# First expert group's rows transposed inside the last two attention chunks, with their buffers placed over the finished k, v and q buffers

## The chip, the cores and the metric

The kernel runs on one core of one Trainium2 chip. The core has five engines: TensorE (PE in the profile), VectorE (DVE), ScalarE (ACT), GpSimd (POOL) and SyncE (SP), and 16 DMA engines that move data. The metric is the device time of one execution in microseconds, lower being better. Time before: a median of 1042.11 us over 3 runs, from 1041.54 to 1044.14.

## What is computed

Two parts, the second on the output of the first. The attention has 8 batches, 8 heads, 576 positions of 64 values; keys and values are averaged over 8 positions first:

```python
k_p = k.reshape(B, H, Sp, pool, D).mean(axis=3)      # pool = 8, Sp = 72
v_p = v.reshape(B, H, Sp, pool, D).mean(axis=3)
scores = scale * np.matmul(q, k_p.transpose(0, 1, 3, 2))
attn = softmax(scores)
x = np.matmul(attn, v_p)                             # laid out as 4608 rows of 512
```

The mixture of experts takes these 4608 rows. A noisy gate picks the best two of 8 experts for each row, and each expert is a network of two layers, 512 to 1024 to 512:

```python
noisy = x @ w_gate + log1p(exp(x @ w_noise)) * noise
top2, top2_w = best two of noisy, softmax over the two
out[row] = sum over its two experts e of  top2_w * (relu(x[row] @ w1[e]) @ w2[e])
```

## The kernel before

**Attention.** A loop runs over 36 chunks of 128 rows: 4 pairs of batches (`pr` 0 to 3), 9 chunks each (`ci`). Chunks belong to units; a unit is two chunks (`jj` 0 and 1) or one. For a chunk `et` (lines 372 to 388) transposes the exponentials on PE (L385, four into a PSUM tile of tag `one`, two into the end of the chunk's accumulator `a`) and copies them on ACT to SBUF (`eT`, L387, with a raised priority); `av` (lines 390 to 428) multiplies with the values (12 matmuls, L399), divides on DVE (`rd` L405 and L406, `xr` L410, `lg` L412) and writes the rows to DRAM (`x_dram`, L417 and L420). Scores of the next unit come from `qk` (L361, maximum L366, exponential L368), and the q rows of the unit after it from `qtr` (L335). The last two chunks, 34 and 35, are the two halves of the last unit; no unit follows, so there is only `et` and `av` in them.

**Routing.** After each 9 chunks `route` (from line 477) works out on DVE and ACT which experts the rows go to, beginning with a sum over the heads (L495), ranks them by matmuls (L568, L572), and queues 18 scatters on POOL (L597) that write row numbers and weights into lists in DRAM (`rec_dram`), one list for each expert. `load_recs` (L612 on) reads lists back (`raw`, L628): the first expert's tiles 0 to 3 after half of the pairs, its tiles 4 to 6 after the third pair, both on POOL's queue, and all the rest on SP's queue once the last pair's scatters have landed. From the last load POOL converts row numbers (`x` L670, `xf` L648), and 16 small matmuls spread them over partitions (`px` and `pw`, L642); they stand in PE's order behind the sixth of the eight blocks of the second group's first layer. Rows are fetched with indirect DMAs on POOL (`xg`, L689 for the first expert).

**Experts.** Each expert's list is worked off in three groups of up to 512 rows. `split` transposes the group's rows (for the first expert on PE, L905, 4 transposes for each of up to 4 tiles of 128 rows) and splits the values into a high part `xh` (ACT cast, first half of L916) and a low part `xl` (DVE subtraction, same line). `stage1` runs 8 blocks (f = 0 to 7) of 12 matmuls (L956) and evicts each with ACT (`hh`, L961) and DVE (`hl`, L962); a matmul reads the columns of all tiles of the group at once. For the first group and f = 0 the matmuls that read `xh` come first (8), then those that read `xl` (4). `stage2` is the second layer (L1060, L1031). Weights are loaded into three staging buffers (`wst`, L446) and split in the same way by `weights` (ACT L467, DVE L468), four steps for a weight tile; a staging buffer is loaded again when its two steps are done.

**The seam.** Two weight tiles of the first expert, `weights(0, 0)` and `weights(0, 1)`, are split during the last pair by the generator `early_w`: eight steps, six in chunks 30 to 32, and the last two behind the loop (`drain(early_w)`). Then the attention's pools close (`att` in SBUF, `ps2` in PSUM), the experts' pools open over the same addresses (`moe`, `mps`, each tile waiting only for the tiles it lies over), and `split(groups[0])` begins. In block f = 0 and after, `hook0` takes up the last pair's `route` and weight tiles 2 and 3. Behind the load of the last of these pieces, on SP's queue, stand 12 writes of zeros to `out` (L936, 768 KB each), and behind those three loads for the second expert's weights and then the late `raw` loads.

**Order.** A planner orders each engine's instructions: by priority, which is the order in which the code traces them, among those whose operands it takes as ready. `tc.issue_after(i)` holds instructions behind `i` on `i`'s engine. Each engine works its own list in order.

Of the kernel before, what the change touches and what calls it, by code (L numbers as in the profile page):

```python
# [20 lines left out]
def kernel(  # L21
# [91 lines left out]
    ctx2 = ExitStack()  # L113
    ap_ = ctx2.enter_context(tc.tile_pool(name="att", bufs=1))
    ps2 = ctx2.enter_context(tc.tile_pool(name="ps2", bufs=1, space=PSUM))
    ps2.tile([P, 512], F32, tag="s", name="s_first", bufs=2)

    ZW = 3
# [88 lines left out]

    def kvload(dst, src, b, nm, nb, np_, parts, acc):

        t = ap_.tile([P, nb, PD], F32, tag=nm, name=f"{nm}{b}", bufs=2)  # L210
        r = src[b].rearrange("h (g t) d -> (h g) (t d)", t=POOL)
        for n0, n1, r0, st in parts:
            def ld(o, w, eng, **kw):
                eng.dma_start(t[:np_, n0:n1, :w], bass.AP(
                    tensor=r.tensor, offset=r.offset + r0 * PD + o,
                    ap=[[PD, np_], [st * PD, n1 - n0], [1, w]]), **kw)
            if acc >> b & 1:
                ld(0, HD, nc.sync)
                accs.append(lambda ld=ld: ld(HD, HD, nc.gpsimd, accum_op=OP.add))
            else:  # L220
                ld(0, PD, nc.sync)
        dst[b] = t
# [25 lines left out]
               [(n, n + 2, VSR[n], VSR[n + 1] - VSR[n]) for n in range(0, NEB, 2)], DV)  # L248

    def load_q(b):  # L250
        t = ap_.tile([P, H, 4, D], F32, tag="q", name=f"q{b}", bufs=2)
        for h in range(0, H, H // (QS if b == 0 else 1)):
            hs = slice(h, h + H // (QS if b == 0 else 1))
            nc.sync.dma_start(t[:, hs].rearrange("p h j d -> p h (j d)"),
                              q[b, hs, :4 * P, :].rearrange("h (p j) d -> p h (j d)", j=4))
        QT[b] = t
        if b % 2 == 0:
            QR[b // 2] = ap_.tile([P, H, D], F32, tag="qr", name=f"qr{b}", bufs=2)
        nc.sync.dma_start(QR[b // 2][b % 2 * 64:b % 2 * 64 + 64],
                          q[b, :, 4 * P:, :].rearrange("h p d -> p h d"))  # L260

    KS, VS, QTT, EX, XR = {}, {}, {}, {}, {}

    def k_prep(b):
        ks = ap_.tile([P, NB, 2, D], F32, tag="ks", name=f"ks{b}")
        KS[b] = ks
        for n0, n1 in ((0, 2), (2, 4), (4, 5)) if b == 0 else ((0, NB),):
            yield from pooled(ks[:, n0:n1], KT[b], n0, n1, P)
# [102 lines left out]
    def et(u, jj):  # L371
        kind, pr, b, jp = u
        nm = f"{pr}_{b}_{jp}_{jj}"
        ex = EX[u][:, jj]
        eT = ap_.tile([P, NEB, P], F32, tag="eT", name=f"eT{nm}", bufs=2)

        a = ps2.tile([P, 2, 512], F32, tag="a", name=f"a{nm}", bufs=AB)
        for n0, n1 in EG:
            if n0:
                ep = a[:, :, 512 - P:]  # L380
            else:
                ep = ps2.tile([P, 512], F32, tag="one", name=f"ep{nm}_{n0}", bufs=2).rearrange(
                    "p (n t) -> p n t", t=P)
            for n in range(n0, n1):
                nc.tensor.transpose(ep[:BST, n - n0], ex[:, ES[n]:ES[n] + BST], ident)  # L385
            with tc.high_priority(offset=HP):
                lastt[0] = nc.scalar.copy(eT[:BST, n0:n1], ep[:BST, :n1 - n0])  # L387
        return eT, a
# [86 lines left out]
    def drain(g):  # L475
        for _ in g:
            pass
# [232 lines left out]
    def one(name):  # L710
        return ps2.tile([P, 512], F32, tag="one", name=name, bufs=2)

    units = []
    for pr in range(NP):
        units += [("D", pr, 2 * pr, 0), ("D", pr, 2 * pr, 1), ("R", pr, 2 * pr, 2),
# [106 lines left out]
    for i, (ui, u, jj) in enumerate(chunks):  # L822
# [5 lines left out]
        if single:  # L828
            order = OR
        else:  # L830
            order = OD[jj]
        eT = None
        def bgs():
            for f in bg.get(i, ()):
# [5 lines left out]
        for o in order + ("" if "b" in order else "b") + ("" if "x" in order else "x"):  # L840
            if o == "v" and i == 0:
                drain(pg[0])
            if o == "b":
                bgs()
            elif o == "x":
                adv()
            elif o == "e":
                eT, at = et(u, jj)
            elif o == "v":
                av(u, jj, ci, eT, at, lgs[pr])  # L850
                lx[i] = lastx[0].ins
            elif o in "012":
                if has:
                    qk(units[ui + 1], int(o))
            elif ui + 2 < NU:
                qtr(units[ui + 2], "qr".index(o))
# [13 lines left out]
            gens.append(route(pr, 0, 5, lgs[pr], one))  # L870
        if ci == NCH - 1 and pr < NP - 1:
            gens.append(route(pr, 5 if pr >= HS else 0, NCH, lgs[pr], one))
    advance(100, 100)
    with tc.issue_after(lastt[0].ins), tc.issue_after(lx[len(chunks) - 2]):
        drain(early_w)
    ctx2.close()


    mctx = ExitStack()
    mp = mctx.enter_context(tc.tile_pool(name="moe", bufs=1, reuse_waits="tile"))  # L880
    pools.append(mp)
    mps = mctx.enter_context(tc.tile_pool(name="mps", bufs=1, space=PSUM, reuse_waits="tile"))

    def w1s(e, hl, db, f):
# [3 lines left out]
        return W[e, 2 + f // 4][:, hl, (f % 4) * DM:(f % 4 + 1) * DM]  # L888

    PASSES = ((0, 0), (0, 1), (1, 0))  # L890
    XT = {}
    SP_ = [None]

    def split(grp):
        e, t0, nt = grp
        xh = mp.tile([P, NDB, 4 * P], F32R, tag="xh", name=f"xh{e}_{t0}")
        xl = mp.tile([P, NDB, 4 * P], F32R, tag="xl", name=f"xl{e}_{t0}")
        for t in range(nt):
            xg = XG.pop((e, t0 + t))
            if e == 0:  # L900
                xp = mps.tile([P, NDB, P], F32, tag="xp", name=f"xp{e}_{t0 + t}", bufs=2) if t0 + t not in (2, 3) else \
                    mps.tile([P, NDB, P], F32, tag="ph", name=f"xp{e}_{t0 + t}", bufs=3)
                xv = xg.rearrange("p (c b) -> p b c", b=NDB)
                for db in range(NDB):
                    nc.tensor.transpose(xp[:, db], xv[:, db], ident)  # L905
                nr = 2 if t0 + t == 9 else 4
                xT = xp.rearrange("p b (r j) -> p b r j", j=32)[:, :, :nr]
            else:
                nr = 2 if t0 + t == 9 else 4
                xt = mp.tile([P, 4, NDB, 32], F32, tag="xt", name=f"xt{e}_{t0 + t}", bufs=2)  # L910
                nc.vector.transpose(xt[:, :nr], xg[:, :nr * P].rearrange("p (r i b) -> p r b i", i=32, b=NDB))
                xT = xt.rearrange("p r b j -> p b r j")[:, :, :nr]
            cs = slice(t * P, t * P + nr * 32)
            xhv = xh[:, :, cs].rearrange("p b (r j) -> p b r j", j=32)
            xlv = xl[:, :, cs].rearrange("p b (r j) -> p b r j", j=32)
            SP_[0] = (nc.scalar.copy(xhv, xT), nc.vector.tensor_sub(xlv, xT, xhv.bitcast(F32)))  # L916
        XT[grp] = (xh, xl)

    HT = {}
    hli = {}  # L920
    evict = []
# [156 lines left out]
                except StopIteration:  # L1078
                    wgens.pop(0)

    with tc.high_priority(offset=LP):
        split(groups[0])
    s0 = SP_[0]
    fetch(groups[1])
    rt = route(NP - 1, 0, NCH, lgs[NP - 1], mone)

# [175 lines left out]
```

## Time and profile before

| What | Value |
|---|---|
| median of 3 runs | 1042.11 us (1041.54 to 1044.14) |
| profiled execution | 1041.25 us |
| its span, first to last instruction | 1039.1 us, so 2.15 us lie around it |
| mean granted TensorE clock | 0.992 |
| PE busy | 1015.6 us, 98% of the span |
| POOL, DVE, ACT busy | 632.6, 560.3 and 338.7 us |
| DMA moved | 140.63 MB, mean 135 GB/s |

A row of the timeline gives start and duration in us, engine, source line, operation, what is written from what, how many were merged, and in brackets the idle time of the engine before it with what ended it. A row of the table of stretches gives the stretch, each engine's busy time in it (with its number of instructions), the granted clock as a share of full speed, the mean busy share of the 16 DMA engines, and GB/s. SPq is SP's queue: there a duration is the time that issuing took, not the transfer.

### The profile page before, as it was taken

The page shows a single profiled execution, that of the slowest core. Times are in us where ns is not written, and L with a number is a line of the kernel's source. Part 1 is how long each engine was busy: PE and PEld are TensorE (multiplying, and loading weights), DVE is VectorE, ACT ScalarE, POOL GpSimd, SP SyncE. Part 2 cuts the span into 40 slices and gives each one's busy share as a digit, 9 for nine tenths or more (in the row PEclk, how much of TensorE's full clock was granted, in tenths as well). Part 3 has the DMA queues.
Part 4 walks back from the last instruction along what each step waited for, and adds up shares of the span by engine and source line. Part 5 has one row for each costly group of instructions (what it writes and reads, how often), then busy time and mean ns, then how long its engine had stood idle before and what let it go on. Part 6 is the DMA issues. An engine that isn't in the chain of part 4 may idle for free. (4 is left out here: it accounts for less than half of the span.)

```text
span 1039.1 us, 16032 instructions
## 1 busy us (share of the span) xinstructions
PE 1015.6 (98%) x5872; PEld 917.8 (88%) x5872; DVE 560.3 (54%) x1284; ACT 338.7 (33%) x857; POOL 632.6 (61%) x661
## 2 busy tenths in 40 slices
PE   6999999999999999999999999999999999999997
PEld 5898998788998998899889988998899889988995
DVE  6898987823464545454545464446444644554331
ACT  5787787412222232123212222222222222222110
POOL 4005476565677677677757775777577757773541
PEclk8999999998999999999999999999999999999999
DMA  9999936796234424442444243423442444232200
GB/s 299 312 329 276 257 82 174 264 213 174 81 92 134 134 65 119 123 141 70 117 130 132 67 123 112 139 72 117 121 124 84 114 122 121 79 93 84 69 19 32
DMA packets 76292, 140.63 MB, mean 135 GB/s; under 512 B 24501, under 2 KB 32778, under 8 KB 76212
## 3 DMA queue, kind: packets, MB, share of 16 engines
q1 hardware_dynamic: 47892, 76.82, 26.3%
q0 software_dynamic: 28320, 62.77, 20.0%
q8 instruction: 47, 0.77, 0.3%
q14 instruction: 33, 0.27, 0.1%
HBM read 102.27 MB, written 39.17 MB: 136 GB/s over the span
## 5 line engine op out<-in xcount | busy, mean ns | idle before, releaser
L956 PE MATMUL ph<-xh,w 128*128 128x384 f32 (+2 forms) x1536 | 405.6, 345 | 0.7 <-ACT xh L916 0.7
L697 POOL DMA_INDIRECT xg<-x_dram,x x266 | 259.3, 975 | 101.9 <-issue 68.9
L956 PEld LDWEIGHTS ph<-xh,w 128*128 128x128 f32 x1536 | 275.7, 188 | 21.2 <-ACT xh L916 0.9
L961 ACT ACTIVATE hh<-ph 128x512 fp32r<-128x512 f32 (+2 forms) x192 | 97.5, 509 | 564.4 <-PE ph L956 564.4
L1060 PE MATMUL py<-w,hh 128*128 128x512 f32 x896 | 276.6, 390 | 0.0
L956 PE MATMUL ph<-xl,w 128*128 128x320 f32 (+2 forms) x768 | 264.5, 345 | 0.0
L962 DVE SCALAR_TENSOR_TENSOR hl<-ph,hh 128x512 fp32r<-128x512 f32 (+2 forms) x192 | 111.0, 579 | 221.9 <-ACT hh L961 221.8
L1060 PEld LDWEIGHTS py<-w,hh 128*128 128x128 f32 x896 | 167.9, 188 | 34.5
L1060 PE MATMUL py<-w,hl 128*128 128x512 f32 x448 | 174.5, 389 | 0.0
L956 PEld LDWEIGHTS ph<-xl,w 128*128 128x128 f32 x768 | 144.7, 188 | 10.3
L998 DVE SCALAR_TENSOR_TENSOR pv<-py,raw,pv 128x128 f32<-128x128 f32 x196 | 54.9, 343 | 131.0 <-PE py L1060 130.4
L1031 PE MATMUL py<-hh,w 128*128 128x320 f32 x512 | 112.8, 309 | 0.0
L1045 POOL DMA_INDIRECT out_dram<-pv,o x80 | 84.6, 1058 | 36.0 <-issue 14.6
L1060 PEld LDWEIGHTS py<-w,hl 128*128 128x128 f32 x448 | 84.1, 188 | 17.4
L1019 POOL DMA_INDIRECT pv<-out_dram,o x70 | 72.4, 1034 | 35.6 <-issue 17.4
L597 POOL DMA_INDIRECT rec_dram<-rec,pos x72 | 74.6, 1036 | 29.5 <-issue 19.2
L1002 POOL DMA_INDIRECT out_dram<-pv,raw x56 | 58.9, 1052 | 53.5 <-DVE pv L998 33.3
L468 DVE TENSOR_TENSOR w<-wst,w 128x512 fp32r<-128x512 f32 x128 | 87.7, 688 | 4.5 <-ACT w L467 4.0
L1031 PEld LDWEIGHTS py<-hh,w 128*128 128x128 f32 x512 | 85.6, 188 | 0.0
L467 ACT CAST w<-wst 128x512 fp32r<-128x512 f32 x128 | 77.2, 615 | 6.4 <-DMA wst<-in_moe_w_dram 3.5
L1031 PE MATMUL py<-hl,w 128*128 128x320 f32 x256 | 79.1, 309 | 0.0
L980 POOL DMA_INDIRECT pv<-out_dram,raw x49 | 50.1, 1022 | 39.4 <-issue 39.4
(157 smaller groups left out, 1003.7 us busy)
## 6 DMA issues: line engine op xcount, KB each, us to landing
wst<-in_moe_w_dram SPq DMA_DIRECT2D x64, 512.0 KB, 3.9
v<-in_v_dram SPq DMA_DIRECT2D x24, 448.0 KB, 11.1
out_dram<-lg SPq DMA_DIRECT2D x12, 768.0 KB, 17.2
k<-in_k_dram SPq DMA_DIRECT2D x7, 1280.0 KB, 13.4
q<-in_q_dram SPq DMA_DIRECT2D x7, 1024.0 KB, 15.0
x_dram<-xr POOLq DMA_DIRECT2D x12, 512.0 KB
xg<-x_dram,x POOLq DMA_INDIRECT x276
x_dram<-xr SPq DMA_DIRECT2D x4, 512.0 KB, 7.0
```

The source lines that it names most:

```text
L467: nc.scalar.copy(hv, sv)
L468: nc.vector.tensor_sub(lv, sv, hv.bitcast(F32))
L597: s = nc.gpsimd.indirect_dma_start(out=rec_dram[:, :], out_offset=bass.IndirectOffsetOnAxis(ap=pos[:, i, c:c + 1], axis=0), in_=rec[:, c, ...
L697: nc.gpsimd.indirect_dma_start(out=xg[:, r * P:(r + 1) * P], out_offset=None, in_=x4, in_offset=bass.IndirectOffsetOnAxis(ap=xi[e, t][:, r ...
L956: nc.tensor.matmul(ph[:, :n], w1s(e, a, db, f), xs[b][:, db, :n], start=(i == 0), stop=(i == 3 * NDB - 1))
L961: ra = nc.scalar.activation(hh[:, :n], ph[:, :n], AF.Relu)
L962: rd = hli[grp, f] = nc.vector.scalar_tensor_tensor(hl[:, :n], ph[:, :n], 0.0, hh[:, :n].bitcast(F32), op0=OP.max, op1=OP.subtract)
L1002: s = nc.gpsimd.indirect_dma_start(out=out, out_offset=bass.IndirectOffsetOnAxis(ap=tokc[e, t][:np_], axis=0), in_=res[:np_], in_offset=No ...
L1019: g = nc.gpsimd.indirect_dma_start(out=pv4[:, i], out_offset=None, in_=out4, in_offset=bass.IndirectOffsetOnAxis(ap=oi4[e, t0 + i // 4][:, ...
L1031: nc.tensor.matmul(py[:, :n], w2s(e, b, f)[:, mb * P:(mb + 1) * P], hs[f][a][:, :n], start=(i == 0), stop=(i == 3 * NFB - 1))
L1045: s = nc.gpsimd.indirect_dma_start(out=out4, out_offset=bass.IndirectOffsetOnAxis(ap=oi4[e, t0 + i // 4][:, i % 4], axis=0), in_=r4[:, i], ...
L1060: lastm[0] = nc.tensor.matmul(py, hs[f][a][:, cs], w2s(e, b, f), start=(i == 0), stop=(i == 3 * NFB - 1))
```

## The change

The buffers for k, v, q and the pooled keys (`k`, `v`, `q`, `qr`, `ks`) move from the pool `att` into a pool of their own, `kvq`, opened after it. When chunk 34 begins, `kvq` closes, and a pool `xpose` opens at the other end of SBUF, for `xh` and `xl` alone. The first group's tile 0 is transposed and split in chunk 34 between `et` and `av`, its tiles 1 to 3 in chunk 35 at the same place; their PSUM tiles carry the attention's tags, `s` (tiles 0 and 1) and `one` (tiles 2 and 3), and no longer the experts'. The two remaining steps of `early_w` are parted: one as before, the other behind the split of tile 3 on ACT and DVE. `split` itself is cut into `xtiles` and `split_tile`, and the later groups use it as before. The diff, cut to its core:

```diff
+    ctx3 = ExitStack()
+    kp = ctx3.enter_context(tc.tile_pool(name="kvq", bufs=1))
...
-        t = ap_.tile([P, nb, PD], F32, tag=nm, name=f"{nm}{b}", bufs=2)
+        t = kp.tile([P, nb, PD], F32, tag=nm, name=f"{nm}{b}", bufs=2)
...
-        t = ap_.tile([P, H, 4, D], F32, tag="q", name=f"q{b}", bufs=2)
+        t = kp.tile([P, H, 4, D], F32, tag="q", name=f"q{b}", bufs=2)
...
-        ks = ap_.tile([P, NB, 2, D], F32, tag="ks", name=f"ks{b}")
+        ks = kp.tile([P, NB, 2, D], F32, tag="ks", name=f"ks{b}")
...
+    def xtiles(grp):
+        return [pools[-1].tile([P, NDB, 4 * P], F32R, tag=w, name=f"{w}{grp[0]}_{grp[1]}") for w in ("xh", "xl")]
+
+    def split_tile(grp, t, xs, xp=None):
+        e, t0, nt = grp
+        xh, xl = xs
+        xg = XG.pop((e, t0 + t))
+        nr = 2 if t0 + t == 9 else 4
+        if e == 0:
+            xv = xg.rearrange("p (c b) -> p b c", b=NDB)
+            for db in range(NDB):
+                nc.tensor.transpose(xp[:, db], xv[:, db], ident)
+            xT = xp.rearrange("p b (r j) -> p b r j", j=32)[:, :, :nr]
...
+        SP_[0] = (nc.scalar.copy(xhv, xT), nc.vector.tensor_sub(xlv, xT, xhv.bitcast(F32)))
...
+        if i == len(chunks) - 2:
+            ctx3.close()
+            pools.append(mctx.enter_context(tc.tile_pool(name="xpose", bufs=1, side="right", reuse_waits="tile")))
+            x0 = xtiles(groups[0])
...
                 eT, at = et(u, jj)
+                for t in {len(chunks) - 2: (0,), len(chunks) - 1: (1, 2, 3)}.get(i, ()):
+                    split_tile(groups[0], t, x0, ps2.tile([P, NDB, P], F32, tag="s" if t < 2 else "one",
+                                                          name=f"xp{t}", bufs=2))
...
+    XT[groups[0]] = x0
+    s0 = SP_[0]
     advance(100, 100)
     with tc.issue_after(lastt[0].ins), tc.issue_after(lx[len(chunks) - 2]):
+        next(early_w)
+    with tc.issue_after(s0[0].ins), tc.issue_after(s0[1].ins):
         drain(early_w)
     ctx2.close()
...
-    pools.append(mp)
+    pools.insert(0, mp)
...
-    with tc.high_priority(offset=LP):
-        split(groups[0])
-    s0 = SP_[0]
```

## Rows read from the trace of the kernel before

**Rows 1.** Timeline of PE, 172 to 200 us, columns as told above: the seam

```profile
175.77 1.78 PE L399 MATMUL a<-vbd,eT 112*128 112x162 f32 x12 [0.46 <-ACT eT L387]
...
178.23 1.78 PE L399 MATMUL a<-vbd,eT 112*128 112x162 f32 x12 [0.46 <-ACT eT L387]
179.84 2.11 PE L905 MATMUL xp<-ident,xg 128*128 128x128 f32 x16
182.65 2.11 PE L956 MATMUL ph<-xh,w 128*128 128x512 f32 x8 [0.70 <-ACT xh L916]
```

**Rows 2.** Timeline of ACT at the seam

```profile
177.80 0.37 ACT L387 COPY eT<-a 112x256 f32<-112x256 f32 x1 [1.38 <-PE a L385]
...
180.54 2.05 ACT L916 CAST xh<-xp 128x512 fp32r<-128x512 f32 x4 [1.33 <-PE xp L905]
```

**Rows 3.** Timeline of DVE at the seam

```profile
177.66 0.17 DVE L405 TENSOR_SCALAR rd<-a 128x8 f32<-128x8 f32 x1 [1.44 <-PE a L399]
...
178.90 1.28 DVE L468 TENSOR_TENSOR w<-wst,w 128x512 fp32r<-128x512 f32 x2
...
181.33 2.47 DVE L916 TENSOR_TENSOR xl<-xp,xh 128x512 fp32r<-128x512 f32 x4
183.72 2.12 DVE L495 TENSOR_REDUCE rt<-lg 128x144 f32<-128x1152 f32 x1
...
190.65 0.22 DVE L534 TENSOR_TENSOR rt<-rt,rt 128x72 f32<-128x72 f32 x1
```

**Rows 4.** Timeline of PE, 150 to 172.5 us: the last transposes of q

```profile
161.59 1.04 PE L335 MATMUL qp<-ident,q 128*128 128x128 f32 x8
```

**Rows 5.** Timeline of PE around 243 us

```profile
243.10 0.78 PE L642 MATMUL px<-xf,sel 128*128 128x80 f32 x3 [2.21 <-POOL xf L648]
```

**Rows 6.** Timeline of POOL, 186 to 275 us

```profile
191.75 0.59 POOL L628 DMA_DIRECT2D raw<-rec_dram  x1 [2.43 <-DMA rec_dram<-rec,pos]
197.33 0.69 POOL L667 TENSOR_SCALAR x<-raw 128x3 int32<-128x3 int32 x1 [4.99 <-DMA raw<-rec_dram]
...
202.29 1.01 POOL L597 DMA_INDIRECT rec_dram<-rec,pos  x1 [0.30 <-DVE cum L1164]
...
225.05 0.96 POOL L597 DMA_INDIRECT rec_dram<-rec,pos  x1 [0.91 <-DMA out_dram<-lg]
...
242.40 0.33 POOL L670 TENSOR_SCALAR x<-raw 128x3 int32<-128x3 int32 x1 [11.53 <-DMA raw<-rec_dram]
242.79 0.25 POOL L648 CAST xf<-raw 128x80 f32<-128x80 int32 x1
```

**Rows 7.** Timeline of SP's queue, 176 to 275 us (issues)

```profile
181.25 0.34 SPq L420 DMA_DIRECT2D x_dram<-xr  x1
190.76 0.37 SPq L446 DMA_DIRECT2D wst<-in_moe_w_dram  x1
191.18 21.91 SPq L936 DMA_DIRECT2D out_dram<-lg  x12
...
235.55 5.02 SPq L628 DMA_DIRECT2D raw<-rec_dram  x4
```

**Rows 8.** Table of stretches, columns as told above: DMA while zeros are written

```profile
193.00:202.00 9.00, 9.00 (x49) 7.30 (x48) 8.72 (x36) 3.87 (x8) 3.76 (x4) 1.00 1.01 379
...
210.00:226.00 16.00, 16.00 (x78) 13.47 (x77) 5.32 (x15) 1.66 (x3) 11.60 (x12) 1.00 1.08 202
```

**Rows 9.** Table of stretches: the clock behind 243 us

```profile
242.00:244.00 2.00, 0.90 (x5) 0.91 (x6) 0.65 (x2) 0.00 (x0) 1.37 (x4) 0.82 0.01 0
244.00:246.00 2.00, 2.00 (x11) 2.00 (x11) 0.55 (x1) 0.00 (x0) 1.45 (x2) 0.50 0.87 72
...
250.00:252.00 2.00, 2.00 (x12) 2.00 (x12) 0.56 (x1) 0.49 (x1) 1.70 (x2) 0.97 0.69 260
```

**Rows 10.** Table of stretches: PE from 243 us to its last matmul

```profile
243.00:1031.00 788.00, 787.90 (x4179) 712.56 (x4180) 374.63 (x749) 184.89 (x360) 524.62 (x522) 1.00 0.35 103
```

**Rows 11.** Timeline of POOL, 157 to 162 us: the first load of a list

```profile
160.37 0.24 POOL L667 TENSOR_SCALAR x<-raw 128x4 int32<-128x4 int32 x1 [0.92 <-DMA raw<-rec_dram]
```

More of the change, by code (lines that the diff above doesn't have):

```diff
@@ L257, in load_q @@
         if b % 2 == 0:
-            QR[b // 2] = ap_.tile([P, H, D], F32, tag="qr", name=f"qr{b}", bufs=2)
+            QR[b // 2] = kp.tile([P, H, D], F32, tag="qr", name=f"qr{b}", bufs=2)
         nc.sync.dma_start(QR[b // 2][b % 2 * 64:b % 2 * 64 + 64],
@@ L711, in one, with split @@
         return ps2.tile([P, 512], F32, tag="one", name=name, bufs=2)
+    mctx = ExitStack()
+    XT = {}
+    SP_ = [None]
+    def xtiles(grp):
[10 more added lines that the diff above has]
+            xT = xp.rearrange("p b (r j) -> p b r j", j=32)[:, :, :nr]
+        else:
+            xt = pools[0].tile([P, 4, NDB, 32], F32, tag="xt", name=f"xt{e}_{t0 + t}", bufs=2)
+            nc.vector.transpose(xt[:, :nr], xg[:, :nr * P].rearrange("p (r i b) -> p r b i", i=32, b=NDB))
+            xT = xt.rearrange("p r b j -> p b r j")[:, :, :nr]
+        cs = slice(t * P, t * P + nr * 32)
+        xhv = xh[:, :, cs].rearrange("p b (r j) -> p b r j", j=32)
+        xlv = xl[:, :, cs].rearrange("p b (r j) -> p b r j", j=32)
+        SP_[0] = (nc.scalar.copy(xhv, xT), nc.vector.tensor_sub(xlv, xT, xhv.bitcast(F32)))
+    def split(grp):
+        XT[grp] = xtiles(grp)
+        for t in range(grp[2]):
+            split_tile(grp, t, XT[grp],
+                       mps.tile([P, NDB, P], F32, tag="xp", name=f"xp{grp[1] + t}", bufs=2) if grp[0] == 0 else None)
     units = []
@@ L872 @@
             gens.append(route(pr, 5 if pr >= HS else 0, NCH, lgs[pr], one))
+    XT[groups[0]] = x0
+    s0 = SP_[0]
     advance(100, 100)
     with tc.issue_after(lastt[0].ins), tc.issue_after(lx[len(chunks) - 2]):
+        next(early_w)
+    with tc.issue_after(s0[0].ins), tc.issue_after(s0[1].ins):
         drain(early_w)
     ctx2.close()
-    mctx = ExitStack()
     mp = mctx.enter_context(tc.tile_pool(name="moe", bufs=1, reuse_waits="tile"))
-    pools.append(mp)
+    pools.insert(0, mp)
     mps = mctx.enter_context(tc.tile_pool(name="mps", bufs=1, space=PSUM, reuse_waits="tile"))
@@ L890 @@
     PASSES = ((0, 0), (0, 1), (1, 0))
[L891 to L917, printed above, removed]
     HT = {}
```

## Prediction

> **What bounds the kernel now.** The page gives PE 98% of the span, so I first ask where PE stands still, in its timeline. There are six idle stretches of over 0.25 us behind 150 us. Three lie at the seam between attention and experts: 0.46 us ahead of chunk 34's `av`, 0.46 ahead of chunk 35's, and 0.70 between the transposes of the first group and its first matmul [rows 1], together 1.62 us. Two more, under 0.5 us each, lie ahead of the seam and are not touched. The last is 2.21 us at 243.1, where the matmul that spreads the row numbers waits for POOL's `xf` [rows 5]. Behind that the table of stretches has PE busy for 787.90 of 788 us [rows 10], and the tail after PE's last matmul hangs on PE. So the end of the kernel is set by **when the matmul at 243.1 may start**. PE's work ahead of it is slack, 2.21 us of it.
>
> What releases that matmul is read backwards. `xf` (242.79) follows the last load of the lists, for which POOL waited 11.53 us [rows 6]. SP issued this load at 235.55, behind the 12 writes of zeros (191.18 to 213.1) [rows 7]. In that time the 16 DMA engines are full: mean busy share 1.01 and 1.08, with 379 GB/s until POOL's scatters begin and 202 GB/s beside them [rows 8]. The release is thus the end of a pile of transfers that starts with the zeros. The zeros follow a weight load (190.76) in SP's order, and that one follows the splitting of the staging buffer, which DVE ends at 190.65 [rows 3, 7].
>
> **The change part by part.** *Transposes on PE.* The 16 transposes take 2.11 us, 0.53 us a tile [rows 1]. They are as many as before. Tile 0 now stands ahead of chunk 34's `av`, and 0.53 us of work meets an idle 0.46 us there. Tiles 1 to 3 (1.58 us) stand ahead of chunk 35's `av`, in its idle 0.46 us. When `av` of chunk 35 is over, the first group's matmuls follow at once, if `xh` is there: chunk 35's `et` transposes ended at 178.23 - 0.46 = 177.77 and end 0.07 later now (0.53 - 0.46), tile 3 is transposed 1.58 us after that, at 179.42, and `av` needs 1.61 us (178.23 to 179.84) up to 181.03. ACT needs 0.51 us a tile [rows 2] and one weight half besides, and is done by 180.5. So the first matmul of the experts moves from 182.65 to 181.03, the whole 1.62 us. The other end: if the planner puts tile 3 behind `av`, the 0.70 stays and 0.92 is gained. I take 1.62, since the transposes come first in the code and need nothing that is late.
>
> *Waits that it adds.* A transposed tile needs its PSUM bank. Tiles 0 and 1 wait for exponentials, tiles 2 and 3 for the copies of `eT`; behind them in PE's order stands only `av`, which waits for the later copy (177.80) [rows 2] anyway. The new SBUF pool lies over k, v, q and `ks`; the last transposes of q ran at 161.59 [rows 4], 12 us earlier, so this costs nothing. The expert buffers slide down by the size of that pool, and weight tile 3 of the first expert lies now over `eT` and `xr`, whose last write to DRAM is issued at 181.25 [rows 7]; `hook0` fills that tile from block f = 2 on, over 8 us later, so I put it at nothing.
>
> *DVE and the start of the zeros.* DVE has no idle time from 177.66 to the routing's first sum at 183.72: two chunks' divisions, two weight halves (1.28 us), four subtractions (2.47 us, 0.62 each) [rows 3]. That work stays. Only tile 0's subtraction can slip into the 1.44 us that were idle ahead of 177.66, so the routing starts 0.62 us earlier; if the second weight half (0.64) falls behind the sum, 1.26. DVE stays busy up to 190.65, so the zeros start earlier by the same 0.62 to 1.26. The staging buffer that this weight half frees is loaded again some 2 us later than before; SP has nothing else due but `xr`'s last write, and the loaded half is used 8 us on, so again nothing.
>
> *The pile of transfers.* A head start of 0.62 us is spent at 379 GB/s (0.23 MB), and saves these bytes later, where the rate is 202 GB/s: 0.62 x 379 / 202 = 1.16 us. With 1.26 it is 2.4. From the other side: POOL's chain (the second early load at 191.75, its row numbers at 197.33, the 18 scatters from 202.29 to 225.05) [rows 6] starts from things that the change doesn't move, so if the last scatter alone decides, the release moves by 0. I take 1.16, because POOL itself waits on DMA at the last scatter (0.91), so the pile decides and not POOL's rate.
>
> **Sum.** PE reaches the waiting matmul 1.62 us earlier, the release comes 1.2 us earlier, the wait grows from 2.21 to 2.6 us, and everything behind it moves by 1.2. The profiled execution (1041.25: 1039.1 of span and 2.15 around it) becomes 1040.05. The median of the runs is 0.86 above that execution, and I keep this distance: **1040.9**. What is not gained is the point: 1.62 us are taken out, and the wait at 243 takes back what the transfers don't follow. I call 0.3%, 3.1 us, the least that measurements of this kernel tell from no change; the forecast lies within it.
>
> **Rivals.** *The release doesn't move.* POOL's chain decides, or DVE's order leaves the zeros where they were. Then the wait grows to 3.8 us and the time is 1042.1, with 1041.5 to 1042.6 around it. For it: every step of POOL's chain stands at its place by earlier waits. Against it: the full DMA engines of rows 8.
>
> *The wait at 243 goes.* If the planner, whose view of PE's time has moved by 1.6 us, puts the spreading matmuls behind another block or two of the first layer, PE never waits: 1.62 + 2.21 = 3.8 us less, 1038.3. [...] Against it: the matmuls stood at the traced place before, with POOL late by 2.2 us, so the planner counts POOL as early.
>
> *Slower: the second early load of a list falls into the zeros.* POOL's first such load cost it a wait of 0.92 us [rows 11], the second, issued 0.6 us behind the first zeros, one of 4.99 [rows 6]. It is issued at 191.75 whatever PE does, while the zeros come earlier by 0.6 to 1.3, so it meets a deeper queue. Each us that it lands later moves row numbers, fetches, all 18 scatters and the release, for POOL has only 0.30 us between these. From a delay of 1.2 us on, the gain above is used up, and beyond that the kernel is slower: a delay of 2.7 gives 1043.6, twice the 4.99 gives 1045.9. [...]
>
> *It doesn't do what it says.* The planner leaves the transposes behind `av`; that is the first rival's time.
>
> **Chances.** Forecast 0.52 (1039.7 to 1041.6, from the bounds 2.4 and 0.6); release unmoved 0.25; wait gone 0.11; slower load 0.12. The range takes in the first two with the spread of the runs, the mild part of the slower load, and the edge of the case without the wait: 1037.8 to 1044.0, which leaves out some 0.15. Faster by over 0.3% (below 1039.0) is the case without the wait and a sliver of the forecast: 0.12. Slower by over 0.3% (above 1045.2) is the far end of the slower load: 0.05. Within 0.3%: 0.83.
>
> **What will show it.** In PE's timeline after: no idle time at 175.8 and 178.2, transposes of the first group ahead of both `av`, the experts' first matmul at 181.0 (181.7 if tile 3 came late). DVE's sum over heads at 182.5 to 183.1, SP's zeros at 190.0 to 190.6, the spreading matmuls at 241.9 with 2.6 us of idle time ahead of them, and a half clock behind it. A release at 243.1 means POOL decides; row numbers of the second early load behind 198.5 mean the slower load; an earlier release with a shorter wait means that I under-counted the pile. A new idle stretch between 181 and 240 would prove the sum wrong as a whole.

## The result, and the profile after

The change makes the kernel slower: 1050.92 us (median of 6 runs, 1049.09 to 1053.83) against 1042.32 for the kernel before beside it, a ratio of 1.0086 with a 95% interval of 1.0071 to 1.0100. The forecast was 1040.9. The profiled execution took 1053.83 us, its span is 1051.7.

The loss doesn't lie where the code was changed. Four points of TensorE's list, present in both profiles, share it out (number 1350 is counted in order of time):

| Point in TensorE's list | before, us | after, us | late by |
|---|---|---|---|
| matmul number 1350, an `av` of the attention, ahead of all moved instructions | 173.14 | 178.37 | 5.23 |
| first matmul of the experts | 182.65 | 185.67 | 3.02 |
| first `px` matmul | 243.10 | 252.02 | 8.92 |
| end of the span | 1039.1 | 1051.7 | 12.6 |

So 5.2 us are lost before the seam, 2.2 are won at it, 5.9 are lost behind it, and 3.7 more in the experts, where nothing was edited. This one profile is worse than the median: 12.6 of span against 8.6 in the medians.

The seam itself, in TensorE's timeline after (L401 is the old L399, L387 the old L385, L972 the old L956). It answers to [rows 1]:

```profile
179.28 0.65 PE L730 MATMUL xp<-ident,xg 128*128 128x128 f32 x4
...
180.82 0.63 PE L730 MATMUL xp<-ident,xg 128*128 128x128 f32 x3 [0.24 <-ACT eT L389]
181.28 1.68 PE L401 MATMUL a<-vbd,eT 112*128 112x162 f32 x12
...
183.01 1.25 PE L730 MATMUL xp<-ident,xg 128*128 128x128 f32 x9
184.10 1.67 PE L401 MATMUL a<-vbd,eT 112*128 112x162 f32 x12
185.67 0.71 PE L972 MATMUL ph<-xh,w 128*128 128x512 f32 x2
```

The 16 transposes stand ahead of the `av` of their chunks, and the three idle stretches of 0.46, 0.46 and 0.70 us are gone; one of 0.24 us is new, ahead of three of the transposes.

Behind it two new ones have come, in the same timeline, and the wait at `px` has grown from the 2.21 us of [rows 5]:

```profile
194.86 0.50 PE L972 MATMUL ph<-xh,w 128*128 128x512 f32 x1 [0.55 <-DVE hl L978]
203.72 0.20 PE L570 MATMUL rk<-mbz,before 128*128 128x80 bf16 x1 [3.00 <-DVE mbz L548]
...
252.02 2.00 PE L644 MATMUL px<-xf,sel 128*128 128x80 f32 x8 [3.64 <-POOL xf L650]
```

The 3.00 us are TensorE waiting for the last pair's router on VectorE. VectorE stood behind ScalarE there, for 1.62 us. ScalarE's timeline and VectorE's, and then SP's issues (to hold against [rows 7]) and POOL's (against [rows 6]):

```profile
200.28 1.14 ACT L469 CAST w<-wst 128x512 fp32r<-128x512 f32 x2 [4.68 <-DMA x_dram<-xr]
```

```profile
187.54 0.69 DVE L412 TENSOR_TENSOR xr<-a,rd 128x512 f32<-128x512 f32 x1
...
200.94 0.69 DVE L470 TENSOR_TENSOR w<-wst,w 128x512 fp32r<-128x512 f32 x1 [1.62 <-ACT w L469]
```

```profile
187.42 0.37 SPq L448 DMA_DIRECT2D wst<-in_moe_w_dram  x1
188.26 0.34 SPq L422 DMA_DIRECT2D x_dram<-xr  x1
196.04 0.37 SPq L448 DMA_DIRECT2D wst<-in_moe_w_dram  x1
```

```profile
197.15 1.03 POOL L599 DMA_INDIRECT rec_dram<-rec,pos  x1 [0.30 <-issue]
208.63 0.59 POOL L630 DMA_DIRECT2D raw<-rec_dram  x1 [10.44 <-DMA rec_dram<-rec,pos]
213.70 0.24 POOL L669 TENSOR_SCALAR x<-raw 128x3 int32<-128x3 int32 x1 [4.48 <-DMA raw<-rec_dram]
```

The cast of weight tile 3 waits for the last write of the rows to DRAM, because that tile lies over `xr` now. The write is issued at 188.26, when VectorE has made the rows (187.54 and 0.69 us), and takes 11.9 us to land. POOL's second early load waits 10.44 us for scatters to land, where it had waited 2.43.

The 3.7 us in the experts show in the table of costliest groups with the shapes kept apart (time busy, mean ns of one). The first layer's matmuls with 512 columns, before and then after:

```profile
L956 PE MATMUL ph<-xh,w 128*128 128x512 f32 x512 | 158.9, 390 | 0.7 <-ACT xh L916 0.7
...
L956 PE MATMUL ph<-xl,w 128*128 128x512 f32 x256 | 99.1, 389 | 0.0
```

```profile
L972 PE MATMUL ph<-xh,w 128*128 128x512 f32 x512 | 162.5, 396 | 0.6 <-DVE hl L978 0.6
...
L972 PE MATMUL ph<-xl,w 128*128 128x512 f32 x256 | 100.9, 396 | 0.0
```

The same 768 matmuls are 263.4 instead of 258.0 us busy, at the same full clock (1.00). From start to start each takes about 233 ns instead of 227, or 22.17 instead of 21.53 us from the first to the last of the 96 of a group: some 0.63 us in each of eight experts, 5.0 us in all. The 384- and 320-column groups have the same length as before (16.5 and 13.9 us from the first start to the last). Behind `px` the end moves by 3.7 and not 5.0: the first expert's 0.63 lies ahead of it, and of the half-clock stretch of [rows 9], 6.8 us in both, 1.6 lie ahead of `px` after, which gives back some 0.8 (an estimate: half of 1.6, at a granted clock of 0.50).

For the 5.2 us ahead of the seam, the table of stretches from 36 to 56 us, when the DMA engines are full with loads of k, v and q (last two columns: busy share of the DMA engines, GB/s). Before, then after:

```profile
36.00:56.00 20.00, 19.81 (x165) 18.96 (x164) 16.78 (x36) 15.06 (x50) 1.43 (x3) 1.00 1.07 312
```

```profile
36.00:56.00 20.00, 19.30 (x159) 18.45 (x160) 14.65 (x31) 15.93 (x53) 1.42 (x2) 1.00 1.07 288
```

The engines are as busy and move 8% less. What that does to TensorE stands in the same profile of the changed kernel: VectorE's timeline, TensorE's, and the table of stretches.

```profile
55.61 1.49 DVE L234 TENSOR_TENSOR k<-k 128x1280 f32<-128x1280 f32 x1 [2.64 <-DMA k<-in_k_dram]
```

```profile
61.66 0.76 PE L363 MATMUL s<-kbd,qT 128*128 128x144 f32 x4 [1.49 <-DVE v L234]
```

```profile
62.60:66.05 3.45, 3.45 (x17) 3.41 (x16) 2.02 (x4) 2.21 (x9) 0.00 (x0) 0.51 1.07 340
```

Between 30 and 80 us VectorE waits 6.0 us in all for loads of k and v; the kernel before has no such wait. TensorE waits for VectorE in turn, is busy for 1.11 of the 2.60 us up to 62.60, and then has a granted clock of 0.51 for 3.4 us, which costs 1.7 by an estimate (half of the stretch). The kernel before has full clock (1.00) from 15 to 243 us.

What the change did to both is to move buffers. In bytes from the start of a partition, `k` began at 92,416 and begins at 153,504; `xh` began at 103,680 and begins at 212,960. The old ones are multiples of 256 bytes; the new ones leave remainders of 160 and 224. `k`, `v` and `q` stood first in the pool `att` and stand now behind all its other tiles, whose 61,088 bytes are no multiple of 256, and `xpose` is counted down from its upper end at 229,344 (212,960 and twice the 8,192 of `xh` and `xl`), which is none either.

### The profile page after: what moved, and what is told of

The parts are those of the page before. It is cut to its first block, busy times and chain, and to the rows that moved or that the text cites. A ratio compares the mean times of both kernels' runs of the same rounds, so it can differ in the third digit from the quotient of the medians.

```text
span 1051.7 us, 16035 instructions
## 1 busy us (share of the span) xinstructions
PE 1021.3 (97%) x5872; PEld 919.2 (87%) x5872; DVE 561.3 (53%) x1284; ACT 338.8 (32%) x857; POOL 632.7 (60%) x661
## 5 line engine op out<-in xcount | busy, mean ns | idle before, releaser
L972 PE MATMUL ph<-xh,w 128*128 128x384 f32 (+2 forms) x1536 | 409.2, 348 | 0.6 <-DVE hl L978 0.6
L972 PEld LDWEIGHTS ph<-xh,w 128*128 128x128 f32 x1536 | 275.6, 189 | 24.3 <-DVE hl L978 1.0
L972 PE MATMUL ph<-xl,w 128*128 128x320 f32 (+2 forms) x768 | 266.6, 348 | 0.0
L972 PEld LDWEIGHTS ph<-xl,w 128*128 128x128 f32 x768 | 144.8, 189 | 11.8
## 6 DMA issues: line engine op xcount, KB each, us to landing
out_dram<-lg SPq DMA_DIRECT2D x12, 768.0 KB, 13.9
```

Source lines behind the costliest of these rows:

```text
L972: nc.tensor.matmul(ph[:, :n], w1s(e, a, db, f), xs[b][:, db, :n], start=(i == 0), stop=(i == 3 * NDB - 1))
```

## The experiments

Theory: the loss is the **place of the buffers** (the remainder that their start leaves when divided by 64, 256 or another power of two), not the order of the work. Rivals: PSUM banks (the first layer's accumulators went from banks 2 to 4 to banks 0 to 2), chance in the attention, and the cover that weight tile 3 lost.

**First round.** The changed kernel again, and three edits of it:

```diff
# a_x64, in the pool xpose, behind xh and xl: both begin 32 bytes lower, as the pool's upper end is fixed
+            pools[-1].tile([P, 8], F32, tag="xpad", name="xpad")
# a_kv64, in the pool att, behind xr and ahead of k, v and q
+            ap_.tile([P, 8], F32, name="apad")
# a_xr, first in the pools att and moe: xr lies under pv4 and yt, which are written late
+    ap_.tile([P, 2, DM], F32, tag="xr", name="xr_first", bufs=4)
...
+    mp.tile([P, 10, NDB, 32], F32, tag="yt", name="yt_first")
```

> The changed kernel once more, for a second profile and a time beside the other runs. Theory A (what the profile of after shows is fixed by where its buffers lie): 1.0086 of the kernel before again (1050 to 1052 us), attention's reference point (the idle gap of TensorE before the first output matmul of the last chunk but one) near 176.7 us, ScalarE's wait for the write of the row tiles near 4.7 us, the TensorE idle near 201 us about 3.0 us, 512-column first-stage matmuls at about 234 ns. Theory B (attention's 5.2 us in that one profile were chance): the ratio is the same, but the reference point falls back to about 171.5 us in this profile and the span is some 5 us shorter than 1051.7.

> The changed kernel with 32 bytes per partition more in the pool of the transposed rows, so that both tiles start at a multiple of 64 bytes as in the kernel before (now 32 over one). Theory alignment: the 512-column first-stage matmuls go from about 234 back to about 227 ns in all eight experts, 8 x 0.63 = 5.0 us less, ratio to before about 1.0038. Rival PSUM banks (the first stage's accumulators lie in other banks since the change, and that is the cause): the step stays at 234 ns and the ratio at 1.0086.

> The changed kernel with 32 bytes per partition more in the attention pool, so that the k, v and q buffers start at multiples of 64 bytes as in the kernel before. Theory alignment of the loads: k lands in about 13.4 us after its issue (16.4 in the profile of after), q in 15.0 (19.6), attention's reference point is back near 171.5 us, ratio 1.0036 to 1.005. Rival chance (the attention's lateness belongs to that one profile): ratio stays at 1.0086, and landings are those of the changed kernel's other profile.

> The changed kernel with the row tiles allocated first in the attention pool and the output tile first in the expert pool, so that the fourth weight tile lies over tiles that nobody reads late, and not over the row tiles that are still being written out. Theory overlay: ScalarE's wait of 4.68 us at the cast of the fourth weight tile and the 3.00 us of TensorE idle near 201 us vanish, the last pair's router starts about 3 us earlier, and the time falls by 1 to 4 us (ratio 1.005 to 1.0077). Rival: the wait vanishes, but the end is set by the scatters, the raw loads and the zeros behind them, which keep their order on their queues; the first product of the last pair stays near 252 us and the time within 0.5 us.

In this round the kernel before took 1302.85 us, for a reason that isn't known (the profile of `a_same` has TensorE busy for 84% of the span and a mean granted clock of 0.90), so the times say little, and the points in time in the expectations can't be compared: ratios of 1.0119 (1.0053 to 1.0185) for the same kernel again, 1.0122, 1.0238 and 1.0176, with intervals of 0.6 to 0.8% to each side. Three things can be read from stretches at full clock. With `k`, `v` and `q` at a multiple of 64 (`a_kv64`) the DMA engines moved 298 GB/s from 36 to 56 us, against 297 in `a_same`. With `xh` at a multiple of 64 the matmul still took 398 ns, so a multiple of 64 did not help here. `a_x64`, one line's instructions in one group (shortest/median/longest in ns, first and last start in us):

```profile
L973 PE MATMUL ph<-xh,w x40: 390/398/502, 237.0 to 251.7; 128*128 128x512 f32 x40
```

And in `a_xr` ScalarE's wait for the rows' write was gone, but TensorE still waited 1.29 us for the router. Whether the place of `xr` is worth time was left to a later round.

**Second round: the remainder or PSUM.**

```diff
# a_x2k: as a_x64, 736 bytes
+            pools[-1].tile([P, 184], F32, tag="xpad", name="xpad")
# a_ps: one PSUM tile ahead of ph
+    mps.tile([P, NDB, P], F32, tag="xp", name="xp_first", bufs=2)
# b_x32, kernel before: 32 bytes ahead of xh and xl, 32 behind them
+            mp.tile([P, 8], F32, name="xpad0")
...
+            mp.tile([P, 8], F32, name="xpad1")
# b_kv32, kernel before: 32 bytes ahead of k, q and v, 32 behind them
+    ap_.tile([P, 8], F32, name="apad0")
...
+    ap_.tile([P, 8], F32, name="apad1")
```

> The changed kernel with 736 bytes per partition more in the pool of the transposed rows, so that both tiles start at the same remainder of 2048 bytes as in the kernel before (1280; it was 2016 in the changed kernel and 1984 with the 32 bytes of the first experiment). Theory place in SBUF, by a larger remainder than 64: the 512-column first-stage matmuls go from about 234 back to about 227 ns, 5.0 us less in all. Rival PSUM banks, and rival distance (the tiles lie at the upper end now): 234 ns stays.

> The changed kernel with one unused PSUM tile ahead of the first stage's accumulators, so that these lie in banks 2, 3 and 4 as in the kernel before (0, 1 and 2 since the change). Theory PSUM banks: the 512-column first-stage matmuls go from about 234 back to about 227 ns, 5.0 us less in all, ratio about 1.0038. Rival place in SBUF: 234 ns stays, ratio 1.0086.

> The kernel before with its transposed rows' two tiles moved by 32 bytes per partition (all other tiles where they were or shifted with whole multiples of 64, PSUM unchanged). Theory place in SBUF: the 512-column first-stage matmuls rise from 227 ns towards 234, up to 5.0 us more, ratio up to 1.005. Rival PSUM banks: 227 ns and ratio 1.000.

> The kernel before with its k, v and q buffers moved by 32 bytes per partition, to the remainder of 64 that they have in the changed kernel. Theory alignment of the loads: k lands about 3 us and q about 4.6 us later after its issue, the attention's reference point goes from 171.4 towards 176.7 us, ratio up to 1.005. Rival chance: landings and ratio as in the kernel before.

Here the kernel before took 1037.68 us (20 runs). Ratios: `a_x2k` 1.0056 (1.0034 to 1.0078), `a_ps` 1.0097 (1.0075 to 1.0119), `b_x32` 1.0083 (1.0068 to 1.0097), `b_kv32` 1.0043 (1.0027 to 1.0058). One expert's first group, the view of one line's instructions, in the order `a_x2k`, `a_ps`, `b_x32`:

```profile
L973 PE MATMUL ph<-xh,w x64: 389/389/395, 301.1 to 322.7; 128*128 128x512 f32 x64
```

```profile
L973 PE MATMUL ph<-xh,w x64: 392/395/397, 306.1 to 328.3; 128*128 128x512 f32 x64
```

```profile
L960 PE MATMUL ph<-xh,w x63: 392/395/397, 295.8 to 317.5; 128*128 128x512 f32 x63
...
L1064 PE MATMUL py<-w,hh x64: 394/394/400, 318.2 to 340.2; 128*128 128x512 f32 x64
...
L1064 PE MATMUL py<-w,hh x64: 389/389/395, 424.6 to 445.9; 128*128 128x512 f32 x64
```

PSUM falls: with the old banks the matmul stays at 395. The place stands in both directions: the old remainder gives 389 back in the changed kernel, and 32 bytes make the kernel before slow. `b_x32` lost 8.65 us, more than the 5.0 expected, and its second layer tells where most of the rest went. The pad behind `xl` moved the hidden rows `hh` and four of the six weight buffers by 64 bytes; the other two lie below the pad, at remainder 0. Where the second layer's weights lie in those two (experts 1, 4 and 7; the second of the three lines is expert 1) it takes 394 ns; where both are moved alike (expert 2, the last line), 389. So in these runs the matmul is slow (394 ns and more, against 389) where its **two operands lie at different remainders**, not where one has a bad address.

`b_kv32` has the loss of the loads: number 1350 at 179.24, and in the table of stretches

```profile
36.00:56.00 20.00, 18.18 (x149) 16.96 (x150) 16.70 (x38) 15.61 (x53) 2.03 (x3) 1.00 1.07 282
```

**Third round: both paddings together, and all tiles moved alike.**

```diff
# a_two: a_x2k and a_kv64.  a_all2: the same and a_xr.  a_kvb: a_kv64 again
# b_all32, kernel before: 32 bytes at the start of the constants' pool
+    cp.tile([P, 8], F32, name="cpad")
```

> The changed kernel with both paddings: 736 bytes in the transposed rows' pool (first-stage matmuls of 512 columns back at 227 ns) and 32 bytes ahead of k, v and q (they start at multiples of 64 bytes). Theory of two places (the loss is 5.0 us of the 512-column matmuls and about 5 us of the loads, and what is left of the seam is between -1.2 and +2 us): the attention's reference point is back near 171.5 us, the 512-column step is 227 ns, ratio 0.999 to 1.002. Rival (a third loss is hidden behind these two): ratio above 1.003.

> Both paddings, and the fourth weight tile kept off the row tiles (they lie under tiles that are written late). Theory overlay: TensorE's idle of 1.4 to 3.0 us between the first matmuls of the last pair's router disappears, the seam's gain of 1.4 to 1.6 us stays, ratio 0.9975 to 0.9995. Rival: the cast waits for another thing instead (the scatters of the third pair, 1.6 us in the run with the larger padding), ratio as with the two paddings alone.

> The changed kernel with the 32 bytes ahead of k, v and q alone. Theory alignment of the loads: attention 4 to 5 us earlier than in the changed kernel, the 512-column step stays at 234 ns, ratio 1.004 to 1.006. Rival (the row tiles or the change itself make the loads slow): ratio 1.009.

> The kernel before with 32 bytes at the start of the constants, so that all tiles behind them move by 32 bytes: transposed rows, hidden rows and all weight tiles have the same remainder again, but 32 over a multiple of 64. Theory relative place (a matmul is slow where its two operands have different remainders of 256 bytes): 227 ns in both stages; only the loads are slow, ratio 1.004 to 1.005. Rival absolute place (32 over 64 is slow for the moving operand by itself): about 234 ns in both stages, over 10 us more, ratio above 1.012.

Ratios: `a_two` 1.0060 (1.0041 to 1.0080), `a_all2` 1.0063 (1.0041 to 1.0084), `a_kvb` 1.0107 (1.0081 to 1.0132), `b_all32` 1.0085 (1.0066 to 1.0104). The matmuls are settled by `b_all32`: both operands of the experts' matmuls lie 32 bytes over a multiple of 256, and they run at full pace:

```profile
L957 PE MATMUL ph<-xh,w x64: 389/389/395, 300.6 to 322.2; 128*128 128x512 f32 x64
```

The rest went against me. `a_two`, `a_all2` and `a_kvb` should have won back the loads and didn't: number 1350 at 176.15, 178.32 (`a_all2`) and 179.74, and 299, 292 and 286 GB/s in the stretch. Multiples of 64 don't do for the loads either; k stood at remainder 192 of 256 in all three. `b_all32` lost more (8.6 us) than the 4.1 of `b_kv32`. Its loads were as slow (282 GB/s, with a granted clock of 0.91 in that stretch). Its pad also moved the staging buffers of the weights and the buffers of the fetched rows, which DMA fills too, to remainder 32; whether that is the rest wasn't tried.

**Fourth round: 256.**

```diff
# a_256: a_x2k, and 96 bytes ahead of k, v and q
+            ap_.tile([P, 24], F32, name="apad")
# a_256r: the same and a_xr.  b_same: the kernel before.  b_kv128: b_kv32 with 128 bytes
```

> The kernel before itself, for a profile on the chip of the other runs. Ratio 1.000. If the remainders of the loads decide, its reference point in the attention (the start of the TensorE matmul number 1350) is at 173 to 174.5 us, as in the two profiles with remainder 0, and its loads move over 305 GB/s between 36 and 56 us; if that was chance it can lie anywhere from 173 to 184.

> The changed kernel with the 736 bytes ahead of the transposed rows, and 96 bytes ahead of k, v and q, which start at multiples of 256 bytes as in the kernel before. Theory remainder of 256: attention's reference point at 173 to 174.5 us, 307 GB/s or more between 36 and 56 us, ratio 1.000 to 1.003 (the seam's gain is spent on the router's wait). Rival (the change itself makes the attention late): 176 to 179 us and ratio 1.006 as with 32 bytes.

> As the run before it, and the row tiles lie under tiles that are written late. Theory overlay: 1 us less than without, ratio 0.998 to 1.002. Rival (the cast then waits for its own load, which lies behind zeros and scatters): the same time as without.

> The kernel before with k, v and q moved by 128 bytes (remainder 128 of 256, 0 of 64). Theory remainder of 256: attention late by 2 to 5 us and ratio 1.002 to 1.0045, as with 32 bytes. Rival remainder of 128 or 64: attention and ratio as in the kernel before.

The kernel before took 1037.22 us (35 runs). `b_same` 1.0003 (0.9995 to 1.0012), `a_256` **1.0011** (1.0001 to 1.0020), `a_256r` **1.0005** (0.9996 to 1.0014), `b_kv128` 1.0026 (1.0014 to 1.0037). The stretch from 36 to 56 us, for `b_same`, `a_256r` and `b_kv128`:

```profile
36.00:56.00 20.00, 19.81 (x165) 18.96 (x164) 16.77 (x37) 14.74 (x51) 1.99 (x3) 1.00 1.07 331
```

```profile
36.00:56.00 20.00, 19.81 (x165) 18.96 (x164) 16.79 (x37) 14.71 (x51) 1.99 (x3) 1.00 1.07 328
```

```profile
36.00:56.00 20.00, 19.30 (x160) 18.21 (x159) 15.81 (x34) 15.67 (x53) 1.42 (x2) 1.00 1.08 284
```

Number 1350 starts at 172.34, 172.31 and 178.16. With multiples of 256 the changed kernel's attention is on time; with 128 it is late. Over the fourteen profiles with a mean granted clock of 0.98 or more, that matmul starts from 172.31 to 174.43 in the five with `k`, `v` and `q` at multiples of 256, of both kernels (`a_256`: 173.10), and from 176.15 to 184.60 in the nine others. The five have a granted clock of 1.00 in each of the six stretches of 20 us from 16 to 136 us; of the nine, eight have one to three of these at 0.76 to 0.98 (`a_two` has none). Over all twenty profiles of this study the seven with k, v and q at multiples of 256 move 305 to 331 GB/s in this stretch (mean 319), the thirteen others 282 to 303 (mean 291), whatever kernel it is. That settles where the loss lies, as both parts come back. Their shares are rougher: by the ratios about 4 us for the matmuls (`a_ps` to `a_x2k`) and 5 for the loads (`a_two` to `a_256`), each with an error of some 2 to 3 us, while in the kernel before the loads alone cost 4.1 (`b_kv32`) and 3.0 us (`b_kv128`).

It also shows the change by itself, without the accident of place. Timelines of `b_same`, TensorE and then VectorE:

```profile
181.86 0.73 PE L956 MATMUL ph<-xh,w 128*128 128x512 f32 x2 [0.70 <-ACT xh L916]
...
195.60 0.21 PE L568 MATMUL rk<-mbz,before 128*128 128x80 bf16 x1
...
240.33 1.12 PE L642 MATMUL px<-xf,sel 128*128 128x80 f32 x8 [0.23 <-POOL xf L648]
```

```profile
182.93 2.12 DVE L495 TENSOR_REDUCE rt<-lg 128x144 f32<-128x1152 f32 x1
...
194.95 0.23 DVE L546 TENSOR_TENSOR mbz<-rt,rt 128x72 bf16<-128x72 f32 x1
```

And `a_256r`, TensorE and VectorE:

```profile
179.59 2.08 PE L977 MATMUL ph<-xh,w 128*128 128x512 f32 x8
...
188.76 0.50 PE L977 MATMUL ph<-xh,w 128*128 128x512 f32 x1 [0.72 <-DVE hl L983]
...
195.90 0.20 PE L571 MATMUL rk<-mbz,before 128*128 128x80 bf16 x1 [1.41 <-DVE mbz L549]
...
240.19 1.01 PE L645 MATMUL px<-xf,sel 128*128 128x80 f32 x8
```

```profile
182.38 2.13 DVE L498 TENSOR_REDUCE rt<-lg 128x144 f32<-128x1152 f32 x1
...
195.62 0.22 DVE L549 TENSOR_TENSOR mbz<-rt,rt 128x72 bf16<-128x72 f32 x1
```

The experts start 2.27 us earlier, and 2.13 us are waited off within the next 16.3: 0.72 for a `hl`, 1.41 for the router's result. At the router's first matmul TensorE is even 0.30 us later than in `b_same`. VectorE begins the router 0.55 us earlier and ends it 0.67 later. Between its two rows stand one `hl` and one weight subtraction more than in `b_same` (four and six against three and five, 0.60 us each from start to start): in VectorE's list, which the planner made, the work of TensorE's earlier blocks goes ahead of the router's steps. VectorE sets the end there. `a_256r` and `a_256` differ in 0.06% with intervals that overlap, so what `xr`'s place costs is not told apart.

**Last round: two weight pieces behind the router.** In the kernel of `a_256r` (`a_rt`) and in the kernel before (`b_rt`) the pieces of weight tiles 2 and 3 go one block later, and the zeros with them.

```diff
-            if f < 4:
+            if 1 <= f < 5:
...
-        if f == 3:
+        if f == 4:
             for i in range(12):
                 zero(i, wld[0, 3, 1])
```

> The changed kernel with the remainders and the row tiles as in the run before last (ratio 1.0005), and in the first expert's first stage the pieces of the third and fourth weight tile go one block of hidden rows later each (and the zeros with them, since they stand behind the last of these loads). Theory VectorE: the last pair's router chain loses two weight pieces of 0.64 us ahead of its end, the wait of 1.4 us on TensorE falls to 0.1 to 0.3 us, the seam's gain comes through as far as the product with px doesn't wait: 0.5 to 1.4 us less, ratio 0.999 to 1.000. Rival (scatters, raw loads and zeros set the end): the wait goes, but px waits as much longer and the ratio stays at 1.0005; or the zeros, 2.7 us later, delay the raw loads behind them and the time rises by up to 2.7 us.

> The same move in the kernel before, whose TensorE doesn't wait for the router. Theory VectorE: nothing to gain on TensorE, ratio 0.999 to 1.000. Rival (scatters set the end): the chain behind the router starts 1.3 us earlier and the kernel before gains as much as the changed one.

The kernel before took 1278.91 us here (mean granted clock 0.92 in the profile of `a_rt` and 0.91 in that of `b_rt`), and the ratios, 0.9990 (0.9939 to 1.0042) and 0.9968 (0.9928 to 1.0009), tell nothing. What the profile of `a_rt` does show, in a stretch at full clock (219 to 246 us), is that the wait on TensorE went:

```profile
240.69 0.21 PE L571 MATMUL rk<-mbz,before 128*128 128x80 bf16 x1
```

The experts' first matmul starts at 225.87 there, 14.8 us ahead of this one, against 16.3 in `a_256r`. That VectorE held the router is shown by this. Whether the 1.4 us then reach the end of the kernel stays open, and so does whether `b_rt` is faster than the kernel before.

## Why the prediction was wrong, step by step

**What bounds the kernel now.** I read [rows 5] and took the wait of 2.21 us at `px` as the bound. A second profile of the same kernel (`b_same`) has 0.23 us there and no half clock behind it. It was one execution's wait, and the sum was built on it.

**Transposes on PE, 1.62 us: right, and under-sized.** The place is as forecast, no idle time directly ahead of either `av`, and counted from number 1350 the experts start 2.2 us earlier in both pairs of profiles (after against before, `a_256r` against `b_same`). The 0.6 us more have no single place: in the starts of `a_256r` and `b_same`, 0.2 us are ahead of chunk 34's `av`, where seven transposes run and not four, 0.2 ahead of chunk 35's, 0.1 behind it, and 0.2 within the two `av`, whose matmuls follow each other a little faster.

**Waits that it adds: the step that failed.** "The new SBUF pool lies over k, v, q and `ks` ... so this costs nothing" asked who waits for whom, and of that it was right: the profile after shows no wait of `xh` or `xl` for k, v, q or `ks`. It didn't ask where the buffers come to lie. Moving `k`, `v`, `q` and `xh`, `xl` to other remainders of 256 bytes costs about 9 us, the whole of the loss within the error. Nothing at the seam names it: the loads move 288 instead of 312 GB/s at the same busy share, with 6.0 us of waits for k and v on VectorE and 3.4 us of half clock over 100 us ahead of the seam, and the matmuls take 396 instead of 390 ns.

For the loads the runs show the size and not the mechanism: 319 GB/s on the mean with `k`, `v` and `q` at multiples of 256, 291 in the other profiles, 9% less, and the least of all, 282, with a remainder of 32 (`b_kv32`, `b_all32`). What the DMA engines do differently there, at a busy share of 1.06 to 1.08 in both, no run shows.

**Weight tile 3 over `xr`: wrong in that profile.** I set the write's issue at 181.25 against a use "over 8 us later", and put the time to its landing at nothing: that was 8.6 us in the kernel before, and 11.9 after. The write was issued 7.0 us later, at 188.26: 5.2 us from the late attention, the rest because the transposes and, on VectorE, the subtractions stand ahead of the division that makes these rows. It landed at 200.2 and the cast began at 200.28, having waited 4.68 us; 1.62 of that came through on VectorE, and with `xr` elsewhere 1.41 of TensorE's 3.00 us remain. That it costs time at the end isn't shown: in `a_256`, with `xr` still there, the cast waits 2.9 us and TensorE 1.4 all the same, and `a_256` against `a_256r` is within the error.

**DVE and the start of the zeros: half right.** The sum over the heads starts 0.55 us earlier in `a_256r`, close to the forecast 0.62. But "DVE stays busy up to 190.65, so the zeros start earlier" treated VectorE's list as fixed. It is the planner's, and with the earlier blocks more work stands ahead of the router. The zeros start at 190.35 against 190.37 in `b_same`: not moved.

**The pile of transfers: not tested by this change,** since the zeros stood still. The release of `px` came 0.9 us earlier in `a_256r` (`xf` at 239.14 against 240.03), and TensorE was there at 240.19, not early any more.

**Sum and rivals.** -1.2 us was forecast; with right remainders the kernel is at +0.05% (-0.04 to +0.14%), +0.5 us, so the seam's gain is spent and the forecast's gain isn't borne out. "The release doesn't move" (1042.1) named about this size, and a wrong place: the gain is lost at the router, 45 us ahead of `px`. The slower rival named the early load behind the zeros; it did come late (213.70 against 197.33), after a wait of 10.44 us for scatters, but the scatters that it waited for were themselves issued late, up to 197.15, behind the first zeros (from 196.45), and its price is within the 5.9 us behind the seam. No rival had the place of the buffers. What I wrote last held: a new idle stretch between 181 and 240 would prove the sum wrong, and there were two.

## What to carry to other kernels

When a change moves buffers, ask where they come to lie, not only who waits for them: print the start of each tile, let buffers that DMA fills start at multiples of 256 bytes (319 against 291 GB/s here), and give the two operands of a matmul the same remainder (389 against 394 to 398 ns here). If the busy share of the DMA engines stays and the GB/s fall (1.07, and 312 to 288, here), or a matmul of the same shape takes 2% longer in stretches that nobody edited (390 to 396 ns here), look at addresses first. And when the busiest engine gains, ask whether the engine that feeds it is full: here 2.13 us of TensorE's 2.27 became waits on VectorE (0.72 and 1.41).

## What the runs showed of the hardware

- A 512-column matmul took 389 ns (227 from start to start) where moving and stationary operand had the same remainder of 256 bytes, and 394 to 398 (231 to 235, 233 on the mean) where they differed: 0 against 224, 192, 32 and, in the second layer, 64 against 0. A common shift by 32 (`b_all32`) or by 64 (`b_x32`, expert 2) cost nothing, 389 ns, nor did a difference of 1,024 (the kernel before, expert 3: 389 ns). Whether the period is 256 or another one (128, 512 or 1,024 fit these runs as well) wasn't tried. With 320 columns a difference changed the pattern of the steps (145 to 150 ns in place of 146 and 147) and not the group's length (13.93 us); with 384 columns one group's matmuls took 336 ns in place of 334, and the group's length stayed (16.5 us).
- With the DMA engines full of loads (busy share 1.06 to 1.08) into SBUF at multiples of 256 bytes, 305 to 331 GB/s were moved (36 to 56 us, seven profiles); at remainders 32, 128, 160 and 192, 282 to 303 (thirteen profiles).
- One profile of the kernel before had 2.21 us of idle time at one matmul with 6.8 us of half clock behind it, another (`b_same`) 0.23 us and none.
